# The unread products of the identity in the first batch's attention steps are left out

## The chip, the cores and the metric

The kernel runs on one core of a Trainium2 chip. The metric is the time of one execution on the device in microseconds; the times below are the median of several runs and the time of one profiled execution. All inputs and the output are in float32.

## The reference

Linear attention over 4 batches, 8 heads, 576 positions and 64 columns of a head, then two feed-forward layers on the 2304 tokens of 512 columns that it gives:

```python
kv = np.einsum('bhsd,bhse->bhde', k, v)
out = np.einsum('bhsd,bhde->bhse', q, kv)
rms = np.sqrt(np.mean(out * out, axis=-1, keepdims=True) + 1e-06)
x = out / rms * g_norm                      # then (2304, 512), tokens by columns
g = x @ w_gate                              # (512, 1536)
x = (g * sigmoid(g) * (x @ w_val)) @ w_out
h = x @ w_in                                # (512, 2048)
return softplus(h) @ w_out2
```

## The kernel before, in words

The kernel is one long program in which each engine's instructions stand in an order fixed when the program is built. A small planner sets that order. A step of TensorE (PE) tells the planner how long it should take (`tick`), and steps of other engines are queued with a due time (`defer`) and are issued when the planner's clock has passed it. Every engine then works through its own queue in order. The change touches no `tick` and no `defer`.

The first batch's attention stands ahead of all else, in 16 steps on PE that `attention_slots(0)` lists: four `kv_step`, four `q_step`, four `o_step` and four `x_step`, one for each pair of heads or each chunk of 128 positions. Their due times stand in `S0` with the shifts of `SHIFT`.

- `kv_step` (line 557 for the 512 full positions, line 568 for the remaining 64) sums k times v of two heads into the PSUM tile kvp, in products with 64 columns. After the last pair, ScalarE (ACT) copies kvp into the tile kv (lines 579, 580).
- `q_step` transposes a chunk of q into pq (line 593); ACT copies it out as qt (line 597). The q of a chunk is first put into order by a copy of ACT or VectorE (DVE) (line 444), which waits for the DMA of q.
- `o_step` multiplies qt by kv into pa (line 611). ACT squares it (sq, line 622), DVE sums it (ss, lines 625 and 626), ACT takes the root (rs, line 628), DVE inverts it (line 634) and multiplies pa by it, which gives x (line 636).
- `x_step` transposes x into px (line 649); ACT makes its high part xh (line 655) and DVE its low part xl (line 658).

Between these, ACT and DVE turn the first tiles of w_gate and w_val into pairs of high and low parts: gz and vz (line 490 on ACT, lines 493, 494, 498 on DVE), then gh, vh and gl, vl (lines 509 and 512). Loads are issued by SyncE's queue from the start of the program on, in a fixed order: k, v, q and the first weights of the first batch come first.

With the first xh, the first products of the feed-forward layer begin (pg and pv, line 690). From there on TensorE has a dense stream of products of 512 columns, into which the attention of the other three batches is woven; the rest of the program is the two feed-forward layers, in sums of three products of high and low parts.

`occupy(at)` (line 540) is called at the start of each kind of step with a name made of the step's letter, batch and number. If the table `OCCUPY` (line 60) has the name, it issues so many products of the identity with itself into the PSUM tile `spare`, which nothing reads. Each such product of float32 is two pieces on PE in the trace, with a weight load each. The table has five names, all of the first batch: `k00` is ahead of the first `kv_step`, `r00` ahead of that step's remaining positions, `q00` ahead of the first transpose of q, `x00` and `x01` ahead of the transposes of the first two chunks of x. The tile `spare` is allocated once from the pool `po`, which has three PSUM banks and is otherwise used by the products of the feed-forward layers.

Of the kernel before, what the change touches and what calls it, by code (L numbers as in the profile page):

```python
# [56 lines left out]

OCCUPY = {"k00": 10, "r00": 5, "q00": 7, "x00": 5, "x01": 2}  # L60

ADD1 = 0.31
ADD2 = 0.1
# [251 lines left out]
def tile_linear_attention_two_ffn(  # L315
# [224 lines left out]
    def occupy(at):  # L540

        if at in OCCUPY:
            if not spare:
                spare.append(po.tile([P, P], F32, tag="po", name="spare"))
            for _ in range(OCCUPY[at]):
                nc.tensor.matmul(spare[0], lhsT=ident, rhs=ident, start=True, stop=True)
# [1232 lines left out]
```

## Time and profile before

| | us |
|---|---|
| median of 3 runs | 887.54 (887.23 to 887.84) |
| the profiled execution's own time | 888.28 |
| its span, from the first to the last instruction | 886.5 |
| TensorE busy | 870.6 |
| VectorE busy | 625.0 |
| ScalarE busy | 366.4 |
| GpSimd busy | 295.0 |

The time of an execution is a little more than the span of its instructions. PE stands for products on TensorE and PEld for its weight loads, which overlap them; POOL is GpSimd. A row of the timeline merges like instructions that follow each other: start, time from the first's start to the last's end, engine, line and operation, and in brackets the idle time of the engine before it and what ended that. Since products overlap, a run's time is less than the count times the duration of one.

### The profile page before, as it was taken

Reading aid. Unit: us, or ns where it says so; the run is one execution under the profiler, and the core shown is the slowest. Engines: PE = TensorE matmul, PEld = TensorE weight load, DVE = VectorE, ACT = ScalarE, POOL = GpSimd, SP = SyncE. Lnnn points to the kernel's source line nnn. Section 1 sums busy time; section 2 is a strip of 40 time slices with the busy share of each in tenths; the row PEclk is TensorE's granted clock in tenths of the full one; section 3 lists DMA queues with packets and bytes.
Section 4 is the critical chain, followed back from the end, with each engine's and each line's share of the span. In section 5 each row is a group of like instructions: output and inputs, shape, how many; then the busy total and the mean of one; then the engine's idle time right before and its main releaser. Section 6 shows DMA issues by size and latency. Waiting matters only on the chain.

```text
span 886.5 us, 12733 instructions
## 1 busy us (share of the span) xinstructions
PE 870.6 (98%) x4744; PEld 735.5 (83%) x4744; DVE 625.0 (71%) x981; ACT 366.4 (41%) x647; POOL 295.0 (33%) x225
## 2 busy tenths in 40 slices
PE   7899999999999999999999999999999999999998
PEld 6677788888888788788888778888888888999986
DVE  1856455978888968989845747788687767776533
ACT  3644535334334333443422544544564333344311
POOL 0333301333533264452321544344523121322212
PEclk9999999999999999999999999999999999999999
DMA  9974202147145234513502346786768755444103
GB/s 259 284 195 76 92 1 81 43 140 241 45 143 178 83 107 153 192 67 114 200 1 72 114 171 217 250 283 237 252 227 297 256 190 190 164 133 150 56 23 119
DMA packets 89902, 135.05 MB, mean 152 GB/s; under 512 B 20592, under 2 KB 51568, under 8 KB 89584
## 3 DMA queue, kind: packets, MB, share of 16 engines
q1 hardware_dynamic: 89536, 134.11, 46.9%
q8 instruction: 37, 0.61, 0.3%
q14 instruction: 25, 0.20, 0.1%
q10 hardware_dynamic: 304, 0.13, 0.1%
HBM read 98.04 MB, written 36.18 MB: 151 GB/s over the span
## 4 chain that ended last, share of the span: by engine, by line
PE 81%; DVE 10%; issue 2%; DMA 2%; ACT 2%; POOL 1%; SPq 1%; DVEq 0%; POOLq 0%; ACTq 0%
PE pz L690 14%; PE pv L690 13%; PE pg L690 13%; PE hY L690 9%; PE py L690 6%; PE hZ L690 5%; PE dY L690 4%; PE pY L690 4%; PE hX L690 2%; DVE yacc L844 2%; PE hr L690 2%; PE dZ L690 2%; PE pa L611 1%; PE pZ L690 1%; DMA vr<-in_moe_w_val_dram 1%
## 5 line engine op out<-in xcount | busy, mean ns | idle before, releaser
L690 PE MATMUL hY<-b,wh 128*128 128x512 f32 x384 | 97.9, 391 | 0.0
L690 PE MATMUL pg<-xh,gh 128*128 128x512 f32 (+1 forms) x240 | 90.1, 375 | 0.0
L690 PE MATMUL pv<-xh,vh 128*128 128x512 f32 (+1 forms) x240 | 89.9, 375 | 0.0
L1472 DVE TENSOR_TENSOR zacc<-zacc,pz 128x512 f32<-128x512 f32 x85 | 57.5, 683 | 44.9 <-PE pz L690 44.8
L690 PE MATMUL pg<-xl,gh 128*128 128x512 f32 (+1 forms) x240 | 88.6, 369 | 0.1
L690 PE MATMUL pg<-xh,gl 128*128 128x512 f32 (+1 forms) x240 | 88.6, 369 | 0.0
L690 PE MATMUL pv<-xh,vl 128*128 128x512 f32 (+1 forms) x240 | 88.5, 369 | 0.0
L690 PE MATMUL pv<-xl,vh 128*128 128x512 f32 (+1 forms) x240 | 88.4, 369 | 0.0
L690 PEld LDWEIGHTS hY<-b,wh 128*128 128x128 f32 x384 | 70.7, 188 | 14.0 <-DVE c L1323 0.2
L774 POOL TENSOR_TENSOR ulc<-u,uhc 128x512 fp32r<-128x512 f32 x36 | 51.1, 1424 | 92.6 <-ACT uhc L771 61.4
L1287 POOL TENSOR_TENSOR gl<-c,gh 128x512 fp32r<-128x512 f32 x37 | 49.9, 1351 | 63.5 <-ACT gh L1285 49.9
L747 ACT ACTIVATE s<-pg 128x512 f32<-128x512 f32 (+1 forms) x50 | 27.7, 554 | 85.0 <-PE pg L690 82.8
L771 ACT CAST uhc<-u 128x512 fp32r<-128x512 f32 x64 | 38.9, 617 | 56.7 <-DVE u L783 48.0
L690 PEld LDWEIGHTS pg<-xl,gh 128*128 128x128 f32 x240 | 45.2, 188 | 8.2 <-DVE xl L658 0.6
L690 PE MATMUL pz<-ph,gl 128*128 128x512 f32 x132 | 51.5, 390 | 0.4 <-POOL gl L1287 0.4
L690 PEld LDWEIGHTS pv<-xl,vh 128*128 128x128 f32 x240 | 45.2, 189 | 7.6
L690 PE MATMUL pz<-pl,gh 128*128 128x512 f32 x132 | 51.4, 389 | 0.0
L690 PE MATMUL pz<-ph,gh 128*128 128x512 f32 x132 | 51.4, 389 | 0.0
L690 PEld LDWEIGHTS pg<-xh,gh 128*128 128x128 f32 x240 | 45.3, 189 | 7.1 <-ACT xh L655 0.2
L690 PEld LDWEIGHTS pv<-xh,vh 128*128 128x128 f32 x240 | 45.3, 189 | 6.9 <-issue 0.2
L690 PEld LDWEIGHTS pv<-xh,vl 128*128 128x128 f32 x240 | 45.3, 189 | 6.6
L690 PEld LDWEIGHTS pg<-xh,gl 128*128 128x128 f32 x240 | 45.3, 189 | 6.6
(264 smaller groups left out, 2228.2 us busy)
## 6 DMA issues: line engine op xcount, KB each, us to landing
wh<-w2d SPq DMA_DIRECT2D x32, 512.0 KB, 5.0
wh<-w2d SPq DMA_DIRECT2D x64, 256.0 KB, 4.4
ir<-in_moe_w_in_dram SPq DMA_DIRECT2D x16, 512.0 KB, 4.0
w2d<-kh SPq DMA_DIRECT2D x32, 256.0 KB, 2.9
pr<-in_moe_w_out_dram SPq DMA_DIRECT2D x16, 512.0 KB, 6.4
gr<-in_moe_w_gate_dram SPq DMA_DIRECT2D x12, 512.0 KB, 5.2
vr<-in_moe_w_val_dram SPq DMA_DIRECT2D x12, 512.0 KB, 6.2
or<-in_moe_w_out_dram SPq DMA_DIRECT2D x12, 512.0 KB, 5.9
```

The source lines that it names most:

```text
L611: nc.tensor.matmul(pv[p0:p0 + n, hp, :], lhsT=qt[:, hp, p0:p0 + n], rhs=kvm[bb][:, hp, :], start=True, stop=True,)
L690: nc.tensor.matmul(dst, lhsT=a, rhs=b_, start=first and i == 0, stop=last and i == n - 1, skip_group_check=not check)
L747: nc.scalar.activation(s[0], pg, AF.Silu)
L771: nc.scalar.copy(hl[0], src)
L774: (nc.gpsimd if en(f"{key}.e", default) == "g" else nc.vector).tensor_sub(hl[1], src, f32(hl[0]))
L844: nc.vector.tensor_add(a[:, d, :], a[:, d, :], p)
L1287: (nc.vector if 0 <= n < len(GLO) and GLO[n] == "v" else nc.gpsimd).tensor_sub(lo, l, f32(hi))
L1472: defer(ADD2, lambda: nc.vector.tensor_add(av[:, m, :], av[:, m, :], p))
```

## The change

The table of the spare products is emptied. `occupy` is still called but issues nothing, and the tile `spare` is not allocated. 29 products fall away, 58 pieces in the trace with 58 weight loads. All other instructions stay, in the same order on every engine.

```diff
-OCCUPY = {"k00": 10, "r00": 5, "q00": 7, "x00": 5, "x01": 2}
+OCCUPY = {}
```

## Rows read from the trace of the kernel before

**Rows 1.** The page: busy time by engine; the granted clock in 40 slices.

```profile
PE 870.6 (98%) x4744; PEld 735.5 (83%) x4744; DVE 625.0 (71%) x981; ACT 366.4 (41%) x647; POOL 295.0 (33%) x225
...
PEclk9999999999999999999999999999999999999999
```

**Rows 2.** The chain of waits, 0 to 60 us: start, us, what.

```profile
9.48 10.19 DMA vr<-in_moe_w_val_dram
...
30.81 1.27 ACT xh L655 x2
```

**Rows 3.** Timeline of PE, 0 to 60 us, like instructions merged.

```profile
1.36 4.63 PE L546 MATMUL spare<-ident 128*128 128x128 f32 x20 [1.36 <-POOL ident masks.py:199]
6.74 0.69 PE L557 MATMUL kvp<-v,k 128*64 128x64 f32 x16 [0.75 <-DMA v<-in_v_dram]
7.36 1.38 PE L546 MATMUL spare<-ident 128*128 128x128 f32 x10
9.80 0.33 PE L568 MATMUL kvp<-kvr,kvr 64*64 64x64 f32 x4 [1.06 <-DMA kvr<-in_v_dram]
...
10.94 1.83 PE L546 MATMUL spare<-ident 128*128 128x128 f32 x14
13.15 1.09 PE L593 MATMUL pq<-ident,q 128*128 128x128 f32 x8 [0.38 <-ACT q L444]
15.48 0.66 PE L593 MATMUL pq<-ident,q 128*128 128x128 f32 x4 [1.24 <-ACT q L444]
16.07 0.69 PE L557 MATMUL kvp<-v,k 128*64 128x64 f32 x16
...
17.82 0.66 PE L593 MATMUL pq<-ident,q 128*128 128x128 f32 x4
18.84 3.81 PE L611 MATMUL pa<-kv,qt 128*128 128x128 f32 x32 [0.36 <-issue]
22.49 1.28 PE L546 MATMUL spare<-ident 128*128 128x128 f32 x10
25.20 0.66 PE L649 MATMUL px<-ident,x 128*128 128x128 f32 x4 [1.43 <-DVE x L636]
25.69 0.61 PE L546 MATMUL spare<-ident 128*128 128x128 f32 x4
26.89 0.66 PE L649 MATMUL px<-ident,x 128*128 128x128 f32 x4 [0.59 <-DVE x L636]
...
30.11 1.09 PE L649 MATMUL px<-ident,x 128*128 128x128 f32 x8
...
32.12 0.50 PE L690 MATMUL pg<-xh,gh 128*128 128x512 f32 x1
```

**Rows 4.** The tile spare, 0 to 6 us: ns of one, min/median/max.

```profile
L546 PE MATMUL spare<-ident x20: 421/421/579, 1.4 to 5.6; 128*128 128x128 f32 x20
```

**Rows 5.** The tile spare, 7 to 28 us.

```profile
L546 PE MATMUL spare<-ident x38: 275/275/377, 7.4 to 26.0; 128*128 128x128 f32 x38
```

**Rows 6.** Timeline of PE, instructions within 2 to 3 us.

```profile
1.73 1.49 PE L546 MATMUL spare<-ident 128*128 128x128 f32 x6
```

**Rows 7.** Timeline of ACT, 12 to 24 us.

```profile
13.84 1.07 ACT L597 COPY qt<-pq 128x512 f32<-128x512 f32 x2 [0.74 <-PE pq L593]
14.80 0.63 ACT L444 COPY q<-qr 128x512 f32<-128x512 f32 x1
...
18.00 0.37 ACT L579 COPY kv<-kvp 64x256 f32<-64x256 f32 x1 [0.32 <-PE kvp L568]
...
19.69 0.67 ACT L490 ACTIVATE vz<-vr 128x512 f32<-128x512 f32 x1 [0.33 <-DMA vr<-in_moe_w_val_dram]
...
23.11 0.21 ACT L628 ACTIVATE rs<-ss 128x8 f32<-128x8 f32 x1 [0.71 <-DVE ss L626]
```

**Rows 8.** What PE waited for, 60 us to the end: us in total, times, longest.

```profile
PE pz L690 <- POOL gl L1287: 1.1, 2, 0.7
...
PE hr L690 <- DMA wh<-w2d: 0.7, 2, 0.5
```

## The prediction

> **What bounds the kernel now.** I read the page first, then the chain of waits of the first 60 us, then the instructions of TensorE (PE) and ScalarE (ACT) in order of time, last PE's own waits. The page says that PE is busy 98% of the span and that the granted clock is full in every slice [rows 1]. So from the moment PE has its dense stream, at about 32 us, the kernel is PE's: whatever moves the start of that stream moves the end, unless a later wait swallows it. Outside the start, PE's waits on other engines and on DMAs are six kinds that make 3.5 us in all, none longer than 0.7 us; the one on a transfer, the only kind that would not move with the kernel, is 0.7 us in all [rows 8]. The change lies wholly ahead of 32 us, and there the chain is another: it runs through the load of the first w_val tile, which lands at 19.66, the ACT step vz at 19.69, the three VectorE (DVE) steps behind it, the norms, x, and then PE's px and ACT's xh [rows 2, 3, 7]. The dense stream cannot begin before xh.
>
> **What the removal takes out.** 29 calls, 58 pieces on PE and as many weight loads. They stand in five runs, and each ends before the real product behind it can start, which waits for something else: 1.36 to 5.99, then 0.75 of waiting for the DMA of v; 7.36 to 8.74, then 1.06 for the DMA of kvr; 10.94 to 12.77, then 0.38 for ACT's q; 22.49 to 23.77, then 1.43 for DVE's x; 25.69 to 26.30, then 0.59 for DVE's x [rows 3]. All are covered, so the direct gain is nothing: none of the real products moves forward, since none waited for PE. If one of these covers were gone the gain would still be at most its own run, but transfers and DVE don't depend on the spare products. No engine reads them, no wait is added and no DMA is moved. The bank that they held is one of three of its pool, first wanted after 32 us, so it frees nothing.
>
> **What they did for the clock.** The page prints a full granted clock from the first slice on [rows 1], but the first 20 spare pieces say otherwise: each lasts 421 ns at the median where the later 38 last 275 [rows 4, 5]. Their spacing is (1.49 - 0.421) / 5 = 0.214 us [rows 6]. Between the run of 10 and that of 14 it is (1.83 - 1.38) / 4 = 0.112 us [rows 3]. The ratio is 1.9, so I read the first 4.63 us as the lower level, 1.2 GHz, and all that follows as 2.4 GHz. What PE did before the clock rose was 4.6 us of unbroken products. Without them PE does nothing until 6.74, and its first unbroken stretch of several us begins with the transposes pq of the third chunk, at 15.48 [rows 3]. Before that, between 6.74 and 15.5, there are only short pieces with idle time of 0.4 to 2.5 us between them. So I take the real work up to there, and some way beyond, at the lower level.
>
> **What that costs, step by step.** (a) kvp of heads 0 and 1, from 6.74 to 10.94: nothing. Its second half waits for kvr to 9.80, lasts 1.1 us and would last some 2.2, which ends at 12.0; the next product waits for ACT to 13.15 [rows 3]. (b) pq of the first two chunks: 8 pieces in 1.09 become 7 x 0.214 + 0.42 = 1.92, so +0.8. ACT's two qt follow them at once, and the copy of q for the third chunk stands behind those in ACT's queue [rows 7]: it too is 0.8 later, and pq of the third chunk begins at 16.3 instead of 15.48. (c) Its four pieces take 0.86 and end at 17.15. kvp of heads 2 and 3 ran from 16.07 to 17.82, 1.75 us, on the 64-column form, of which no row shows the lower level. Bounds: 1.75 unchanged if it isn't the array's clock that sets it, 1.75 x 1.9 = 3.3 if it is. I take 3.3, because the spare products, the nearest row, scale so in both their parts. kvp then ends at 20.5 instead of 17.82, +2.65. (d) ACT's kv copies start at 18.0 + 2.65 = 20.65 and end at 21.4; pq of the fourth chunk ends at 20.5 + 3 x 0.214 + 0.42 = 21.5; its qt runs from 21.6 to 22.2; vz, which stands behind it, starts at 22.2 instead of 19.69. It had waited 0.33 for its DMA [rows 7], which is absorbed. So vz is +2.5, and with it all of DVE's chain. With kvp unchanged the same sum gives +0.6. (e) pa starts at 21.5 instead of 18.84. If the clock is full by then, its third chunk is done at 24.4, and ACT's rs, which stands behind the third sq, is ready earlier than DVE's sum that it waits for, so nothing is added to 2.5. If it stays at the lower level for 4.6 us more, the third chunk is done at 26.5, its sq at 27.1, and rs starts there instead of at 23.11 [rows 7]: +4.1 in place of 2.5. By the row of the start, 4.6 us of unbroken work, the clock is full at 16.3 + 4.6 = 20.9, before pa. So I take +2.5 and keep 4.1 for the range. (f) From the first x on everything is shifted as a block: px of the second chunk waits for x [rows 2, 3], and from there PE is dense. Absorbed later: at most the 0.7 us of waits on DMAs [rows 8]; I take nothing.
>
> The sum, +2.5, is against the profiled execution's own time of 888.28 us (its span is 886.5): 890.8. The median of the runs shown is 887.54, 0.74 lower, so as a median 890.0 (+0.28%).
>
> **Rivals.** *The clock is full before 16 us.* Then only (b) is paid: +0.8 at pq of the third chunk, less the 0.33 that vz had waited, so +0.5: 888.0, which cannot be told from no change. It decides if the short pieces between 9.8 and 15 us, which get longer at the lower level (2.2 and 1.9 us of some 5), raise the clock as the unbroken run did. For it: with the spares the stretch 13.15 to 16.07 was far from full and the clock held. Against it: that was holding, not raising, and nothing was dense. Chance 0.15.
>
> *The clock falls again between pa and px.* With pa ending near 25.2 and the first px at 25.20 + 2.5 = 27.7, and the second at 29.4, PE has some 0.5 us of work in 4.2 us; before, the two runs of 10 and 4 spare pieces lay there [rows 3]. Then the path from the second px (26.89) to the end of the last (31.20), 4.3 us of PE work without a break, runs at the lower level: if 4.6 us of it raise the clock again, these hold 4.6 / 1.9 = 2.4 us of full-clock work, and 2.2 are lost; all of it would lose 4.3 x 0.9 = 3.9. Total 2.5 + 2.2 = 4.7, to 6.4 at most: 892.2. Against it: no single pause of PE there would be longer than some 2.5 us, and the clock held through the pauses of 1.4 us that stand there now. Chance 0.25.
>
> The Trainium skill (TensorE: Matmul & The Clock Gate, Part 4: PE-mode transpose) says that transposes don't count as PE work for the clock as products do. By that rule px would not break the pause, which is this last rival, and pq would not help to raise the clock before pa either. The transposes do run at the full clock here (8 pieces in 1.09 us [rows 3]); whether they hold or raise it no row of before shows.
>
> *The 64-column products don't slow down.* +0.6 to +2.2, by the sum with 1.75 in (c), the upper end if pa runs at the lower level: 888.1 to 889.7. Chance 0.06. *Faster* would need a real product that waited for a spare one, and the rows show none; 0.02 for what I don't see, such as another order of code loading.
>
> **How the numbers follow.** The forecast, the lower level until about the start of pa, has 0.52 and gives 890.0, with a range of its own from 889.4 to 891.7 by (e). The range 888.1 to 893.2 leaves out most of the first rival and the far end of the second, under 2 in 10 together. A measurement of this kernel can tell about 0.2%, or 1.8 us. Slower by more than that: the forecast, the falling clock, and half of the 64-column case, 0.80; within it: the first rival and the other half, 0.18; faster 0.02.
>
> **What would show it.** In the profile after: the first kvp still begins near 6.74 and px still waits for DVE. pq of the first two chunks takes about 1.9 us instead of 1.09; kvp of heads 2 and 3 about 3.3 instead of 1.75; ACT's vz starts near 22.2 and no longer waits for its DMA; the first dense product pg near 34.6 instead of 32.12. The first rival shows kvp at 1.75 and pg near 32.6. The second shows px and the kvp between them at twice their time again, and pg near 36.8. The forecast is wrong if pg's start and the end don't move by the same amount, that is, if something behind 32 us absorbs it.

## The result and the profile after

The changed kernel takes 891.60 us (median of 3 runs, 891.55 to 893.25) against 887.54, 0.46% more from median to median; the ratio over all runs is 1.0054 with a 95% interval of 1.0034 to 1.0074. Here and below, three single executions of 1076 to 3054 us (one of the kernel before, two of variants) are left out. The profiled execution is one of 891.60, with a span of 889.8 us. The profiled execution of before was 888.28, with a span of 886.5, so from trace to trace the difference is 3.3 us; the other 0.74 is that the profiled execution of before lay that much above its median.

The page of the kernel after, span and busy time of the engines:

```profile
span 889.8 us, 12617 instructions
...
PE 867.3 (97%) x4686; PEld 731.6 (82%) x4686; DVE 625.2 (70%) x981; ACT 366.6 (41%) x647; POOL 295.0 (33%) x225
```

There are 116 instructions less (58 on PE, 58 weight loads) and DVE, ACT and POOL do what they did [rows 1]. PE has only 3.3 us less of busy time, although the spare pieces had filled five runs of 9.7 us together [rows 3]: the rest came back as longer real products.

The timeline of PE in the kernel after, 0 to 62 us, the lines that answer to [rows 3]:

```profile
6.85 1.12 PE L557 MATMUL kvp<-v,k 128*64 128x64 f32 x16 [6.85 <-DMA v<-in_v_dram]
9.49 0.48 PE L568 MATMUL kvp<-kvr,kvr 64*64 64x64 f32 x4 [1.52 <-DMA kvr<-in_v_dram]
...
12.92 1.94 PE L593 MATMUL pq<-ident,q 128*128 128x128 f32 x8 [1.49 <-ACT q L444]
16.05 1.11 PE L593 MATMUL pq<-ident,q 128*128 128x128 f32 x4 [1.19 <-ACT q L444]
17.09 1.12 PE L557 MATMUL kvp<-v,k 128*64 128x64 f32 x16
...
20.02 1.11 PE L593 MATMUL pq<-ident,q 128*128 128x128 f32 x4
21.04 5.65 PE L611 MATMUL pa<-kv,qt 128*128 128x128 f32 x32
28.48 0.66 PE L649 MATMUL px<-ident,x 128*128 128x128 f32 x4 [1.78 <-DVE x L636]
30.17 0.66 PE L649 MATMUL px<-ident,x 128*128 128x128 f32 x4 [1.04 <-DVE x L636]
...
33.39 1.09 PE L649 MATMUL px<-ident,x 128*128 128x128 f32 x8
...
35.40 0.50 PE L690 MATMUL pg<-xh,gh 128*128 128x512 f32 x1
```

Every real product ahead of 21 us takes 1.5 to 1.8 times what it took: kvp 1.12 for 0.69, its remaining positions 0.48 for 0.33, pq of two chunks 1.94 for 1.09. pa takes 5.65 us for 3.81. At a spacing of 0.214 us for the first n pieces and 0.112 for the others, 32 pieces take 5.65 where n is 19: the clock went from 1.2 to 2.4 GHz about 4.0 us into pa, at 25.0. From the first px on all is as before, later by one and the same amount: px of the second chunk 30.17 for 26.89, pg 35.40 for 32.12, both +3.28, and the span +3.3. Nothing behind 35 us gives any of it back.

What set the 3.28 is in the chain of waits of the kernel after, 0 to 60 us:

```profile
3.24 8.89 DMA qr<-in_q_dram
...
17.16 1.05 PE kvp L557 x16
...
21.13 3.67 PE pa L611 x16
24.83 0.61 ACT sq L622
25.46 0.70 DVE ss L625
```

Before, the chain went through the load of the w_val tile and ACT's vz [rows 2, 7], and DVE began its first sum straight behind its steps on vz (timeline of DVE before):

```profile
22.19 0.68 DVE L625 TENSOR_REDUCE ss<-sq 128x8 f32<-128x512 f32 x1
```

Now the chain starts at the load of q and runs through PE: pq, kvp, pq and the first 16 pieces of pa, that is its first two chunks. An engine that was covered has become the bound of this stage, with its clock at the lower level.

### The profile page after: what moved, and what is told of

The parts are those of the page before. It is cut to its first block, busy times and chain, and to the rows that moved or that the text cites. A ratio compares the mean times of both kernels' runs of the same rounds, so it can differ in the third digit from the quotient of the medians.

```text
span 889.8 us, 12617 instructions
## 1 busy us (share of the span) xinstructions
PE 867.3 (97%) x4686; PEld 731.6 (82%) x4686; DVE 625.2 (70%) x981; ACT 366.6 (41%) x647; POOL 295.0 (33%) x225
## 4 chain that ended last, share of the span: by engine, by line
PE 85%; DVE 8%; issue 2%; ACT 2%; POOL 1%; DMA 1%; SPq 0%; DVEq 0%; POOLq 0%; ACTq 0%
PE pv L690 14%; PE pz L690 14%; PE pg L690 14%; PE hY L690 9%; PE py L690 6%; PE hZ L690 5%; PE pY L690 4%; PE dY L690 4%; PE hX L690 2%; PE hr L690 2%; PE dZ L690 2%; PE pa L611 2%; PE pZ L690 2%; DVE yacc L844 2%; DMA qr<-in_q_dram 1%
```

## The experiments

The theory: the spare products matter through TensorE's clock alone. Without them the real products of the first batch run at 1.2 GHz until pa, and some executions lose the clock again between pa and px. The rivals: their number, their place in the code or the bank that they hold matter; or vz, not pa, sets DVE's chain. All experiments keep all of the reference's computation.

### The changed kernel again

Edit: none.

> The changed kernel again, more often. Theory (the clock): the first three runs were 891.6, 891.55 and 893.25 with mean granted clocks 0.999, 1.000 and 0.995, so the time should come in steps that go with the mean clock: most near 891.6, a few near 893.3, and none below 890. Rival (the spare products matter in another way, by their number or by the place that the code takes): one time for all runs, no link to the mean clock.

Measured: 890.24, 891.24, 891.70, 891.88 at a mean clock of 0.999 to 1.000, and 893.84 at 0.996; ratio to before 1.0051 (1.0038 to 1.0064). The lower group is wider than I had said, from 890.2 to 891.9 at one mean clock, but the slowest is again the one with the lower mean clock, and no run of the changed kernel is as fast as the median of before. The kernel before shows the same in itself: of 17 executions beside these, 12 took 886.6 to 888.5 us and the five of 889.05 to 890.71 have mean clocks of 0.994 to 0.998.

### Only the first 10 products

```diff
-OCCUPY = {"k00": 10, "r00": 5, "q00": 7, "x00": 5, "x01": 2}
+OCCUPY = {"k00": 10}
```

> Only the 10 products ahead of the first k step stay, 19 of 29 are left out. Theory (the clock): these raise the clock at 6 us as before; if it then holds through the pauses between 7 and 16 us the time is 887.5 to 888, if it falls there the first x is late by as much as in the changed kernel, 890.5 to 891.6. Either way kvp of heads 2 and 3 shows the level: 1.75 us at the full clock, 2.9 at the lower one. Rival (the number of instructions): 19/29 of 4.1 us more, 890.2, at a full clock.

Measured: 891.51, ratio 1.0045 (1.0032 to 1.0059). The first kvp in the timeline of PE, then stretches of the same trace: start and end, length, the busy time and instructions of PE, PEld, DVE, ACT and POOL, the granted clock, the share of the DMA engines and GB/s.

```profile
7.00 0.69 PE L557 MATMUL kvp<-v,k 128*64 128x64 f32 x16 [1.52 <-DMA v<-in_v_dram]
```

```profile
5.00:8.00 3.00, 1.17 (x21) 0.87 (x19) 0.00 (x0) 0.00 (x0) 0.00 (x0) 1.00 0.89 211
8.30:12.00 3.70, 1.94 (x24) 1.55 (x24) 0.00 (x0) 0.00 (x0) 0.00 (x0) 0.50 1.08 329
...
21.00:25.00 4.00, 4.00 (x20) 4.00 (x20) 1.81 (x3) 1.99 (x4) 0.00 (x0) 0.50 1.09 349
25.40:30.00 4.60, 2.09 (x17) 1.66 (x16) 4.01 (x11) 1.73 (x6) 0.00 (x0) 1.00 1.16 289
```

The clock was raised, the first kvp took 0.69, and by 8.3 it was back at half, 1.2 GHz, after PE had waited 1.5 us for v and while it waited 1.8 for kvr. It stayed there to 25. So the first run alone buys nothing, the time is that of the changed kernel: what the other runs add here is that the level holds.

### Without the 7 products ahead of px

```diff
-OCCUPY = {"k00": 10, "r00": 5, "q00": 7, "x00": 5, "x01": 2}
+OCCUPY = {"k00": 10, "r00": 5, "q00": 7}
```

> The 7 products ahead of the transposes px are left out, 22 stay. Theory (the clock): the level is full from 6 us to the end of pa, so px of the second chunk starts at 26.9 as before. If the clock holds through the pause between pa and px the time is 887.5; if it falls there in some executions those are later by 1.7 to 2.2 us, 889.3 to 889.8, at a mean clock near 0.997. Rival (the number of instructions): 7/29 of 4.1 us more in all runs, 888.5.

Measured: 889.62, ratio 1.0023 (1.0012 to 1.0033); six of seven between 889.54 and 890.34 at mean clocks of 0.994 to 0.996, one at 887.84 and 1.000. So two steps as the theory had it, with the fall the rule. Timeline of PE, then the stretches around it:

```profile
18.34 3.81 PE L611 MATMUL pa<-kv,qt 128*128 128x128 f32 x32 [0.36 <-issue]
24.27 0.66 PE L649 MATMUL px<-ident,x 128*128 128x128 f32 x4 [2.11 <-DVE x L636]
25.96 1.12 PE L649 MATMUL px<-ident,x 128*128 128x128 f32 x4 [1.04 <-DVE x L636]
27.01 1.12 PE L557 MATMUL kvp<-v,k 128*64 128x64 f32 x16
...
31.39 1.97 PE L649 MATMUL px<-ident,x 128*128 128x128 f32 x8
...
34.75 0.72 PE L690 MATMUL pg<-xh,gh 128*128 128x512 f32 x1
```

```profile
22.00:25.00 3.00, 0.81 (x6) 0.42 (x4) 2.55 (x8) 0.42 (x2) 0.00 (x0) 1.00 1.09 349
25.00:27.00 2.00, 1.04 (x4) 0.72 (x4) 1.79 (x6) 1.21 (x3) 0.00 (x0) 0.50 1.10 350
...
33.00:35.20 2.20, 2.20 (x23) 1.68 (x22) 1.83 (x3) 2.02 (x3) 0.00 (x0) 0.50 1.09 354
35.20:38.00 2.80, 2.66 (x15) 1.72 (x15) 0.90 (x3) 2.71 (x6) 0.00 (x0) 0.99 0.70 186
```

pa ran at the full level, the clock fell at 25, behind waits of 2.1 and within one of 1.0 us, and did not come back before 35.2 although PE was busy without a break from 25.96 on. From px of the second chunk to pg it took 8.8 us instead of 5.2 [rows 3]. That is the prediction's second rival, in a kernel of its own. Not all of these 3.6 us reach the end: in this execution both px start 0.93 us earlier than before, and the wait of 0.57 us for q that PE had behind the first pg products is gone.

### Without the first 10 products

```diff
-OCCUPY = {"k00": 10, "r00": 5, "q00": 7, "x00": 5, "x01": 2}
+OCCUPY = {"r00": 5, "q00": 7, "x00": 5, "x01": 2}
```

> Only the 10 products ahead of the first k step are left out, the 19 others stay. Theory (the clock): nothing raises the clock by 6 us. The runs of 5 and 7 products then stand at the lower level (2.1 and 3.0 us) with the k step between; if they raise it before 16 us the loss is what the transposes pq and the lengthened runs cost until then, +0.5 to +1.0: 888 to 888.5; if they don't, kvp of heads 2 and 3 takes 2.9 us and the time is 890 to 891.6. Rival (the number of instructions): 10/29 of 4.1 us more, 888.9, with kvp at 1.75.

Measured: two groups, five of 11 executions at 887.11 to 887.65 and six at 889.29 to 890.09, all at mean clocks of 0.999 to 1.000; ratio 1.0008 (0.9996 to 1.0021), not told from no change. The trace is of the slower group:

```profile
7.10 1.12 PE L557 MATMUL kvp<-v,k 128*64 128x64 f32 x16 [7.10 <-DMA v<-in_v_dram]
8.15 2.50 PE L546 MATMUL spare<-ident 128*128 128x128 f32 x10
10.59 0.48 PE L568 MATMUL kvp<-kvr,kvr 64*64 64x64 f32 x4
...
12.46 3.35 PE L546 MATMUL spare<-ident 128*128 128x128 f32 x14
15.60 1.41 PE L593 MATMUL pq<-ident,q 128*128 128x128 f32 x8
...
18.84 0.69 PE L557 MATMUL kvp<-v,k 128*64 128x64 f32 x16
```

The first products are the part that can nearly be spared: with the runs of 5 and 7 the clock is up before 18 us. In this execution that was within the pq at 15.60, where 8 pieces take 1.41 us, between 1.09 and 1.94. Where that is late they stand in the way themselves: pq starts at 15.60 and no longer waits for q, 2.4 us later than with a full clock [rows 3]. No execution here shows a lower mean clock for this; the likely reason is that the page counts the time before the first recorded rise as full, as it did in [rows 1].

### Transposes in place of the first products

```diff
-            for _ in range(OCCUPY[at]):
+            for _ in range(2 * OCCUPY[at] if at == "k00" else 0):
+                nc.tensor.transpose(spare[0], ident, ident)
+            for _ in range(0 if at == "k00" else OCCUPY[at]):
                 nc.tensor.matmul(spare[0], lhsT=ident, rhs=ident, start=True, stop=True)
```

> The 10 products ahead of the first k step become 20 transposes of the identity, the same PE time; the 19 other products stay. Theory 1 (transposes don't raise the clock): the first kvp is at the lower level, 1.12 us, and the times are those of the kernel that leaves the 10 products out, two groups near 887.3 and 889.8 with a median near 889. Theory 2 (they raise it as products do): the first kvp takes 0.69 and the times are those of the kernel before, 887.6.

Measured: 887.34, ratio 1.0006 (0.9995 to 1.0017). The first kvp is read from the trace of a second run of the same kernel:

> The kernel with 20 transposes in place of the 10 first products once more, for a profile of an undisturbed execution: its times so far, 886.3 to 890.7 with a median of 887.3, are those of the kernel before. If the transposes raise the clock as products do, the first kvp takes 0.69 us and the clock is recorded as full from between 4.5 and 7 us on. If not, the first kvp takes 1.12, and the times were equal for another reason.

Measured: 887.91, ratio 1.0000 (0.9985 to 1.0016). Timeline of PE:

```profile
1.36 4.53 PE L546 MATMUL spare<-ident 128*128 128x128 f32 x20 [1.36 <-POOL ident masks.py:199]
6.85 0.69 PE L559 MATMUL kvp<-v,k 128*64 128x64 f32 x16 [0.97 <-DMA v<-in_v_dram]
...
27.03 1.12 PE L651 MATMUL px<-ident,x 128*128 128x128 f32 x4 [0.59 <-DVE x L638]
```

The transposes raised the clock: kvp takes 0.69. (In this execution, of 890.81, the clock was down again by the px at 27.03, although the 7 products were in place.)

### Products of 64 columns in place of the first products

```diff
-            for _ in range(OCCUPY[at]):
+            for i in range(32 if at == "k00" else 0):
+                nc.tensor.matmul(spare[0][64 * (i % 2):64 * (i % 2) + 64, 0:64], lhsT=ident[:, 0:64], rhs=ident[:, 0:64], start=True, stop=True)
+            for _ in range(0 if at == "k00" else OCCUPY[at]):
                 nc.tensor.matmul(spare[0], lhsT=ident, rhs=ident, start=True, stop=True)
```

> The 10 products ahead of the first k step become 32 products of the form of kvp, 64 by 64 columns in the two halves in turn, about the same PE time at the lower level; the 19 others stay. Theory 1 (this form doesn't raise the clock, as the unbroken 5 us of pq and kvp ahead of pa didn't in the changed kernel): first kvp 1.12 us, median near 889. Theory 2 (it raises the clock): first kvp 0.69 us, 887.6; then it was the transposes that kept the clock low ahead of pa.

Measured: 890.39, ratio 1.0032 (1.0019 to 1.0045), and the first kvp took 1.12. But the 64 pieces had lasted only 3.7 us, less than the 4.0 to 4.6 of the other kernels, so neither theory was settled, and the next variant has 44 of them.

```diff
-            for i in range(32 if at == "k00" else 0):
+            for i in range(44 if at == "k00" else 0):
```

> As the kernel with 32 products of 64 by 64 columns ahead of the first k step, but with 44, so that their unbroken run lasts 5.0 to 5.1 us, longer than the 4.0 to 4.6 us after which the products and the transposes of 128 columns had raised the clock (32 of them lasted only 3.7). Theory 1 (this form doesn't raise the clock): every piece still lasts 314 ns and the first kvp 1.12 us. Theory 2 (3.7 us were merely too short): the last pieces last 222 ns or the first kvp takes 0.69 us, and the time is 887.5.

Measured: 890.35, ratio 1.0031 (1.0014 to 1.0048). Timeline of PE, then the tile spare from 0 to 7 us:

```profile
1.36 4.57 PE L546 MATMUL spare<-ident 128*64 128x64 f32 x88 [1.36 <-POOL ident masks.py:199]
6.88 0.69 PE L559 MATMUL kvp<-v,k 128*64 128x64 f32 x16 [0.96 <-DMA v<-in_v_dram]
...
15.08 0.70 PE L595 MATMUL pq<-ident,q 128*128 128x128 f32 x4 [1.24 <-ACT q L444]
16.44 1.12 PE L559 MATMUL kvp<-v,k 128*64 128x64 f32 x16 [0.66 <-DMA v<-in_v_dram]
```

```profile
L546 PE MATMUL spare<-ident x88: 222/314/370, 1.4 to 5.7; 128*64 128x64 f32 x88
```

The last pieces last 222 ns and kvp 0.69: this form too raises the clock, and theory 1 of the two expectations is false. The 887.5 us of theory 2 did not come either, as the time was lost later: the granted clock is full from 13.8 to 15.5 us and half from 15.6 to 16.4, so it fell within the pq at 15.08, which stands behind a wait of 1.24 us for q that the kernel before has too [rows 3]. A wait of 0.66 us for v then follows that the kernel before did not have. The kernel with 32 of them has the same wait (0.65), and there the clock fell behind it, within the kvp that follows; whether the new work causes the wait or the fall, no run tells.

### The same instructions with hardly any work

```diff
-                nc.tensor.matmul(spare[0], lhsT=ident, rhs=ident, start=True, stop=True)
+                nc.tensor.matmul(spare[0][:, 0:1], lhsT=ident, rhs=ident[:, 0:1], start=True, stop=True)
```

> All 29 products stay, each with one column of the identity instead of 128, so that the instructions, their weight loads, their place and the tile spare are those of the kernel before and only the work in each product is gone. Theory (the clock): the level stays low until pa, kvp of heads 2 and 3 takes 2.9 us, and the time is that of the changed kernel, 891 to 892. Rival (the number of instructions, their weight loads, the bank or the place of the code): 887.6.

Measured: 893.45, ratio 1.0070 (1.0054 to 1.0085). The rival of number, bank and place falls: with all 29 products there, in the same places, the gain of having them is gone. I had expected 891 to 892; the rest is in the timeline of PE:

```profile
8.19 2.29 PE L546 MATMUL spare<-ident 128*128 128x1 f32 x10
10.42 0.48 PE L568 MATMUL kvp<-kvr,kvr 64*64 64x64 f32 x4
...
12.29 3.14 PE L546 MATMUL spare<-ident 128*128 128x1 f32 x14
15.30 1.95 PE L593 MATMUL pq<-ident,q 128*128 128x128 f32 x8
```

A piece of one column is hardly shorter than one of 128 at this level (3.14 for 14, against 3.35 in the kernel without the first 10), probably for its weight load, which is the same. So the two runs delay pq to 15.30, where the changed kernel starts it at 12.92, and px of the second chunk is still 1.5 us late against it (31.63 for 30.17). The profiled execution, of 894.97, also lost the clock again within that px.

### vz ahead of the qt of the fourth chunk

Against the changed kernel, cut to the entry of the table `SHIFT` that differs:

```diff
-    'wv.0': 1.71
+    'wv.0': -1.5
```

> The changed kernel with the ACT step vz moved ahead of the qt of the fourth chunk, so that it starts 0.6 to 0.7 us earlier than there, just behind the kv copies. Theory 1 (as the prediction's step d had it, vz sets DVE's chain): the first sum ss and px come 0.6 to 0.7 us earlier after the start of pa than in the changed kernel, and the time is 0.6 lower, 891.0. Theory 2 (pa at the lower level sets it; DVE's first sum is that of the second chunk, which waits for that chunk's pa): DVE's wait ahead of the first sum grows from 1.2 to 1.9 us, px starts 7.4 us after pa as there, and the time stays 891.6.

Measured: 893.54, ratio 1.0060 (1.0039 to 1.0081). DVE's first sum in the kernel after, then in this one (timelines of DVE):

```profile
25.46 0.69 DVE L625 TENSOR_REDUCE ss<-sq 128x8 f32<-128x512 f32 x1 [1.23 <-ACT sq L622]
```

```profile
21.98 0.43 DVE L493 TENSOR_SCALAR vz<-vz 128x512 int32<-128x512 int32 x1 [1.40 <-ACT vz L490]
...
25.51 0.69 DVE L625 TENSOR_REDUCE ss<-sq 128x8 f32<-128x512 f32 x1 [1.65 <-ACT sq L622]
```

vz came 0.68 earlier against the start of pa, and DVE only waited longer, 1.65 us for 1.23. px starts 7.18 us after pa, for 7.44, and that 0.26 is pa's own: the clock rose earlier in it, so that its first 16 pieces took 3.41 us for 3.67 and the whole 5.28 for 5.65. So vz doesn't set the chain; theory 2 holds. The time was not 891.6 but higher, at a mean clock of 0.996 in all four executions; the stretches in the trace show where, the granted clock falling behind px:

```profile
24.50:31.20 6.70, 3.77 (x39) 3.18 (x40) 5.00 (x13) 2.82 (x7) 0.00 (x0) 1.00 1.14 296
31.30:38.00 6.70, 6.70 (x80) 5.55 (x74) 4.02 (x8) 3.69 (x7) 2.96 (x3) 0.50 0.84 269
```

This is what the executions of 893 to 894 of the changed kernel should look like, which have the same mean clock; none of them was profiled. Why it is the rule here and the exception there stays open.

### More products

```diff
-OCCUPY = {"k00": 10, "r00": 5, "q00": 7, "x00": 5, "x01": 2}
+OCCUPY = {"k00": 10, "r00": 5, "q00": 7, "x00": 8, "x01": 4}
```

> The kernel before with 8 and 4 products ahead of px instead of 5 and 2; by its trace the longer runs still end before x is there. Theory (its executions of 889 to 890.7, 9 of 44 so far, lose the clock in the pause between pa and px, as the kernel without these 7 products does in most): they vanish, all runs between 886.3 and 888.5, the median 887.2. Rival (they lose it elsewhere, or the longer runs cost something themselves, as in the kernel with more products everywhere): the median is 888 to 889 or the spread stays.

Measured: 887.48, ratio 0.9996 (0.9986 to 1.0006); all 11 executions between 886.57 and 888.22, where before had 5 of 20 between 888.6 and 891.2 beside them. The tail goes, as the theory had it. That fits a loss of the clock in the pause between pa and px, such as the trace with the 20 transposes shows, but with 11 executions, and none of the later executions of before profiled, it is not shown. The median does not move. The trace of this kernel shows something else:

```profile
1.36 4.64 PE L546 MATMUL spare<-ident 128*128 128x128 f32 x20 [1.36 <-POOL ident masks.py:199]
6.85 1.12 PE L557 MATMUL kvp<-v,k 128*64 128x64 f32 x16 [0.86 <-DMA v<-in_v_dram]
7.90 2.50 PE L546 MATMUL spare<-ident 128*128 128x128 f32 x10
```

The same 20 pieces as before, as long [rows 3], and here the clock was still low behind them.

```diff
-OCCUPY = {"k00": 10, "r00": 5, "q00": 7, "x00": 5, "x01": 2}
+OCCUPY = {"k00": 11, "r00": 7, "q00": 8, "q02": 4, "x00": 8, "x01": 4}
```

> More of the products: 11 ahead of the first k step, 7, 8, a new 4 ahead of the third transpose of q, 8 and 4 ahead of px, so that hardly a pause of over half a us is left from 7.4 to 27 us (by the trace of the kernel before each run still ends before the real product's operand is there). Theory (the kernel before loses its clock in a pause in some executions, those of 889 to 890.7 at a mean clock of 0.994 to 0.998): these vanish, 886.6 to 888 with a median near 887.2. Rival (those executions come from something else): the same spread as before, 886.6 to 890.7.

Measured: ratio 1.0016 (1.0006 to 1.0026), 887.47 to 890.38. Not better: it is 0.16% slower than before, clear of no change, and its tail of 889 to 890.4 stays, though nearly all executions have a full mean clock. The one profiled is of 888.12 and shows the level full from the first kvp on and no pause of over 0.8 us. A late rise, behind which the longer runs stand in the way as in the kernel without the first 10, would explain the slower ones; this is argued, not shown. Neither of the two versions is faster than the kernel before.

## Why the prediction was right, and where it was short

The sign, the cause and the place were right: the spare products are covered and cost nothing, what they bring is the clock, and the loss of the first 30 us arrives whole at the end. The path by which the lower clock reaches px was another than forecast. The measured 891.6 lies in the range of 888.1 to 893.2, 1.6 above the forecast. Step by step:

- The direct gain of nothing held. Each real product that had waited behind a spare run still waits: kvp for v, kvr and q for their loads, px for x. kvp even begins at 6.85 for 6.74.
- (a) held: the second half of kvp ends at 11.4, and pq starts when ACT has q.
- (b) held in size: pq 1.94 us, 1.92 forecast. pq of the third chunk starts at 16.05, not 16.3, as the load of q landed 0.3 earlier in this execution.
- (c) was a little too large: kvp of heads 2 and 3 takes 17.09 to 20.02, 2.9 us for 1.75, a ratio of 1.67 and not 1.9. The bound of no change for the 64-column form was wrong.
- (d) was too large, mostly by what (c) was, and wrong in its role: vz starts at 21.65, +1.96 for the +2.5 forecast, with no wait for its load left. It no longer sets DVE, as the experiment that moved it shows.
- (e) is the step that failed, twice. I took the clock to be full by 20.9, after 4.6 us of unbroken work counted from 16.3; it rose at 25.0, after 8.9 us of unbroken work. And I let pa act through its third chunk and ACT's rs, where DVE's first sum is that of the second chunk (L625 takes ss of chunk 1 first), which needs only the first half of pa and so needs it early. At the lower level 16 pieces take 3.67 us, the second sq ends at 25.43, and DVE starts its sums at 25.46, where the timeline of before has 22.19: +3.27, which is what arrives at px. The 4.1 that I kept as the upper end was for a clock that stays low in pa, though by way of the third chunk; I chose the lower end by a row of other work. That 887.54 + 4.1 is the measured 891.6 is luck: the traces show 3.28, and the rest is where the profiled execution of before lay.
- (f) held to a hundredth: +3.28 at px, at pg, and 3.3 in the span.
- Of the other 0.74 the prediction had spoken, as the distance of the profiled execution of before from its median; it added 2.5 to the median as if both profiled executions lay alike, and they don't.

The first rival, a clock full before 16 us, is seen in none of the eight executions of the changed kernel (the fastest is 890.24). With the runs of 5 and 7 in place it may come: the kernel without the first 10 has such times in five of its 11 executions (887.1 to 887.7), none of which was profiled. The second rival exists: it is the rule without the products ahead of px (+2.1 us, where the sum said 2.2). The agreement of the two is luck: the sum let the clock come back after 4.6 us, but in the trace it came back only after 9.2 us of it, and nearly the whole stretch from the second px to pg was slow, 3.6 us more, near the 3.9 that the sum had as its other end; other shifts of this execution took some of it back. The rival also fits the executions of 893.25 and 893.84 of the changed kernel.

For the second rival the prediction had named the Trainium skill (TensorE: Matmul & The Clock Gate, Part 4: PE-mode transpose), by which transposes don't count as PE work for the clock as products do. The measurement differs: 20 transposes of the identity, 4.5 us of them with no product among them, raised it, with kvp at 0.69 us behind. That is a test of raising; whether px holds the level less than a product of the same length would, no run tells.

## What to carry to other kernels

An instruction that nothing reads can still be worth its place: before one is taken out, compare what a like instruction lasts early and late in the trace (here 421 ns and 275) and ask which products behind it would move to the longer time. Then follow these to the first queue in which they are awaited, in the order in which that queue really stands. And where the clock can rise or fall at another time in another execution, one profile is one sample: look at the mean clock of all runs before reading a difference of 0.2% from two traces.

## What was not expected of the hardware

- The same work does not raise the clock at the same time. 20 products in 4.0 to 4.6 us were followed by kvp at 0.69 us (the kernel before, the one without the products ahead of px, the one with only the first 10), and in another execution 20 in 4.64 us by kvp at 1.12.
- In the changed kernel the clock stayed at 1.2 GHz through 8.9 us without a pause (pq, kvp, kvr, pq, half of pa); without the products ahead of px through 9.2 us (px, kvp, px, kvp, from 25.96 to 35.2); and in the kernel without the first 10 through some 9 us from 7.10 on, into the pq at 15.60, although 24 pieces of spare products are among them. Transposes alone and products of 64 columns alone had raised it in runs of about 4.5. What in the mix holds it down was not settled; the products with the 64 remaining positions, which have 64 rows, are in all three stretches and were not tried by themselves.
- It falls without a long pause: by 8.3 us behind a wait of 1.5 us, one kvp and part of a wait of 1.8 (the kernel with only the first 10), and at 25 us behind a wait of 2.1 us, one px and part of a wait of 1.0 (the one without the products ahead of px).
- The page shows a granted clock of 1.00 before the first recorded rise, also where the pieces last 421 ns. The level there is to be read from the durations.
